# A PSUM copy moved to ScalarE and a layer norm regrouped, in a fused forward-and-backward kernel

## Chip, cores, metric

The kernel runs on one core of a Trainium2 chip. The metric is the device time of one launch in microseconds, the median of several launches. Engines are named as the profile names them: PE is TensorE (matmuls), PEld its weight loads, DVE is VectorE, ACT is ScalarE, POOL is GpSimd, SP is SyncE, which here issues nearly all DMA transfers (its queue is SPq). PEclk is the granted clock of TensorE, 1.00 being full speed.

## The reference

One layer and all its gradients. A layer norm of `x` (2048 x 1024) feeds two branches: a filter branch that convolves along the sequence by Fourier transforms, and a gated MLP with a hidden size of 3584. The kernel returns the output and nine gradients.

```python
x = A_q
xn = _layernorm(x, axis=-1)                       # (x - mean) / sqrt(var + 1e-5), bf16 steps
out = x + _A_ref(xn, A_k, A_v, A_shift_k, A_ssm_k, A_ssm_D) \
        + _B_ref(xn, B_W_gate, B_W_up, B_W_down)  # h = relu(xn Wg) * (xn Wu); h Wd
# ... and jax.vjp of it with grad_out, for all inputs but B_x
```

Nothing in the reference is special to the change. What matters is the load: the MLP's products keep TensorE full for nearly 2 ms, and the filter branch is threaded through the first half of them, group of 128 channels by group.

## The kernel before

Three places matter. Each group's filter is transposed on TensorE into PSUM and copied to SBUF. The copy is the last line but one, and it is on VectorE (`vcopy`):

```python
def ttile(self, name):
    return self.ts.tile([P, 19, P], BF16, name=name, tag="ts")     # self.ts: a ring of 3 buffers

def h_tile(self, st):
    hT = self.ttile("hT")
    hv = st["hn"][:].rearrange("p r c -> p (r c)").rearrange("p (q r) -> p r q", r=16)
    pst = self.ps.tile([P, 16, P], BF16, name="pst", tag="aps")    # one of 2 PSUM buffers of the branch
    for r in range(16):
        self.pri.now()
        self.nc.tensor.transpose(pst[:, r, :], hv[:, r, :], self.identA[:])
    self.vcopy(hT[:, 0:16, :], pst[:])
    return hT
```

The layer norm is a generator that works on chunks of 1, 1, 2, 2, 2, 4 and 4 tiles of 128 rows. Its steps are interleaved with the MLP's first block. The program is traced in one order, and the queue of each engine is ordered from it when the kernel is built, by priorities and estimates; `keep_in_program_order` pins an instruction behind what was traced before it on its engine.

```python
LN_CHUNKS = (1, 1, 2, 2, 2, 4, 4)

def layer_norm(self, xn_d, jpool, jtag, spool):
    st0 = 0
    for i, n in enumerate(self.LN_CHUNKS):
        ...
        for j in range(n):
            total = row_sums(j, 0, ACT.Copy)          # on ACT
            if i >= 3 and j == 0:
                self.tc.keep_in_program_order(total)
        mean = average(0, b(0))                       # on DVE
        if i == 2:
            self.tc.keep_in_program_order(mean)       # <- this pin matters below
        V.tensor_copy(out=f(1), in_=b(0))
        for j in range(n):
            V.tensor_scalar(out=xt[:, j, :], ..., op0=ALU.subtract)
            row_sums(j, 2, ACT.Square)
        yield                                         # end of step 1
        var = average(2, b(1))
        if i == 1:
            self.tc.keep_in_program_order(var)
        ...                                           # square root on ACT, six small DVE instructions
        self.ln_dve = V.reciprocal(out=self.rstd[:, st0:st0 + n], in_=f(10))
        self.pri.now()
        for j in range(n):
            V.tensor_scalar(out=xt[:, j, :], ..., op0=ALU.mult)
            ...
        yield                                         # end of step 2
```

The start of the MLP uses it so (`flip` transposes normalized tiles on TensorE and copies them from `pst_x` to `xnT` on VectorE):

```python
def chunk():
    next(ln)
    next(ln)

if ahead:
    self.warm(28)      # dummy matmuls
    chunk()            # tile 0
    next(ln)           # tile 1, step 1
    flip(1)            # tile 0: transposes and copy
    next(ln)           # tile 1, step 2
    chunk()            # tiles 2 and 3
    yield from gate_up(0)
    ...
```

## Time and profile before

| | before |
|---|---|
| median of 3 launches | 1957.82 us (1957.11 to 1959.85) |
| profiled span | 1954.1 us, at the fast end of this kernel's launches |
| PE busy | 1919.8 us (98%) |
| PE waits on the filter copy | 9.7 us, 4 times |
| PE waits in the layer norm | 4.5 us in all |

To read it: PE is the bound. The prediction below shows the list of waits. Two more views of this kernel are needed. The first is PE's timeline at the two first products of the MLP (columns: start in us, length in us, engine, line, operation, tiles, shape, count, and in brackets the idle time before it and what ended that):

```profile
11.85 1.90 PE L663 MATMUL ps_g<-wg,xnT 128*128 128x512 bf16 x8 [0.79 <-DVE ln_b L615]
...
15.83 0.39 PE L663 MATMUL ps_g<-wg,xnT 128*128 128x512 bf16 x1 [1.18 <-DVE xnT L689]
```

Tile 0's product starts at 11.85 us and takes 1.90 us for eight matmuls. The second view is the table of stretches (stretch in us, its length, busy time and count of each engine, then PEclk, DMA share and GB/s), around the wait on the filter copy that ends at 847.49:

```profile
core 0: us, PE busy (x) PEld busy (x) DVE busy (x) ACT busy (x) POOL busy (x), PEclk, DMA share, GB/s
...
847.00:850.50 3.50, 3.01 (x22) 1.61 (x22) 3.50 (x5) 1.01 (x1) 0.00 (x0) 0.52 0.09 20
```

PEclk is 0.52 in these 3.5 us: a stretch of half clock, 3.41 us long, begins at 847.11. PE not only stood still for 2.48 us, it also ran at half speed for the 3.0 us that were left of the stretch. The page's slices, 49 us wide, hide this: they show 9 everywhere.

### The profile page before, as it was taken

The page shows a single profiled execution, that of the slowest core. Times are in us where ns is not written, and L with a number is a line of the kernel's source. Part 1 is how long each engine was busy: PE and PEld are TensorE (multiplying, and loading weights), DVE is VectorE, ACT ScalarE, POOL GpSimd, SP SyncE. Part 2 cuts the span into 40 slices and gives each one's busy share as a digit, 9 for nine tenths or more (in the row PEclk, how much of TensorE's full clock was granted, in tenths as well). Part 3 has the DMA queues.
Part 4 walks back from the last instruction along what each step waited for, and adds up shares of the span by engine and source line. Part 5 has one row for each costly group of instructions (what it writes and reads, how often), then busy time and mean ns, then how long its engine had stood idle before and what let it go on. Part 6 is the DMA issues. An engine that isn't in the chain of part 4 may idle for free.

```text
span 1954.1 us, 36167 instructions
## 1 busy us (share of the span) xinstructions
PE 1919.8 (98%) x15530; PEld 884.3 (45%) x15530; DVE 913.0 (47%) x1356; ACT 617.0 (32%) x852; POOL 15.4 (1%) x38
## 2 busy tenths in 40 slices
PE   8989999999999999999999999999999999999998
PEld 4434444444444444444444444444444444444443
DVE  6767668677677566255255435300222222222222
ACT  6544454444444434434444444411000000000000
POOL 1100000000000000000000000000000000000000
PEclk9999999999999999999999999999999999999999
DMA  9975778964775874453663543592999955554451
GB/s 267 237 174 145 186 179 185 210 184 137 168 186 137 211 206 131 141 152 118 191 156 114 138 124 95 135 292 89 254 237 242 209 132 121 122 123 122 121 124 36
DMA packets 615969, 319.08 MB, mean 163 GB/s; under 512 B 450936, under 2 KB 585088, under 8 KB 615808
## 3 DMA queue, kind: packets, MB, share of 16 engines
q1 hardware_dynamic: 605312, 295.79, 60.3%
q10 hardware_dynamic: 9216, 16.78, 2.9%
q0 software_dynamic: 1280, 4.20, 0.6%
q8 instruction: 121, 1.98, 0.4%
q14 instruction: 40, 0.33, 0.1%
HBM read 141.56 MB, written 95.44 MB: 121 GB/s over the span
## 4 chain that ended last, share of the span: by engine, by line
PE 88%; DVE 5%; DMA 3%; issue 2%; SPq 1%; ACT 0%; POOL 0%; DVEq 0%; POOLq 0%; ACTq 0%
PE ps_w L810 19%; PE ps_x L944 19%; PE ps_o L910 10%; PE ps_g L663 9%; PE ps_h L663 8%; PE ps_u L663 8%; PE ps_d L810 8%; PE ps L66 6%; DVE tap L74 1%; DMA out_dram<-gv 1%; DVE flp L304 1%; DVE gk L74 1%; DVE ksh L74 1%; DMA kp<-in_A_k_dram 1%; DMA xn_nat<-xn_d 1%
## 5 line engine op out<-in xcount | busy, mean ns | idle before, releaser
L810 PE MATMUL ps_w<-ugs,xn_nat 128*128 128x512 bf16 x1792 | 400.3, 379 | 2.0 <-DMA xn_nat<-xn_d 1.6
L663 PEld LDWEIGHTS <-xnT 128*128 128x128 bf16 x1792 | 171.0, 98 | 217.6 <-issue 15.0
L810 PEld LDWEIGHTS <-xn_nat 128*128 128x128 bf16 x1792 | 170.7, 98 | 209.7 <-issue 5.9
L663 PE MATMUL ps_g<-wg,xnT 128*128 128x512 bf16 x896 | 207.5, 382 | 8.1 <-DVE ru L734 3.9
L663 PE MATMUL ps_u<-wu,xnT 128*128 128x512 bf16 x896 | 206.8, 381 | 0.0
L663 PE MATMUL ps_h<-wdT,goT 128*128 128x512 bf16 x896 | 205.5, 379 | 0.0
L957 ACT ACTIVATE w<-xn,m 128x512 f32<-128x512 bf16 x32 | 24.3, 806 | 559.5 <-issue 317.2
L944 PE MATMUL ps_x<-wgT,ggT 128*128 128x512 bf16 x896 | 198.6, 379 | 0.0
L944 PE MATMUL ps_x<-wuT,guT 128*128 128x512 bf16 x896 | 198.6, 379 | 0.0
L910 PE MATMUL ps_o<-wd,hT 128*128 128x512 bf16 x896 | 193.6, 379 | 0.0
L810 PE MATMUL ps_d<-g_nat,hs 128*128 128x512 bf16 x832 | 188.9, 382 | 0.0
L304 DVE STREAM_TRANSPOSE flp<-C 128x1024 f32<-128x1024 f32 x48 | 90.8, 1938 | 107.6 <-ACT C L70 107.6
L865 ACT CAST wi<-ps_w 128x512 bf16<-128x512 f32 x112 | 65.5, 586 | 228.7 <-PE ps_w L810 213.2
L944 PEld LDWEIGHTS <-guT 128*128 128x128 bf16 x896 | 87.7, 98 | 105.7
L944 PEld LDWEIGHTS <-ggT 128*128 128x128 bf16 x896 | 87.7, 98 | 105.7
L910 PEld LDWEIGHTS <-hT 128*128 128x128 bf16 x896 | 87.7, 98 | 105.7
L304 DVE STREAM_TRANSPOSE flp<-B 128x1024 f32<-128x1024 f32 x48 | 90.7, 1943 | 94.6 <-ACT B L70 94.6
L663 PEld LDWEIGHTS <-goT 128*128 128x128 bf16 x896 | 85.5, 98 | 103.4 <-issue 3.4
L810 PEld LDWEIGHTS <-hs 128*128 128x128 bf16 x832 | 79.3, 98 | 97.5 <-issue 6.5
L946 DVE CUSTOM_DVE_ANT_0 gx<-ps_x,gy 128x512 f32<-128x512 f32 x32 | 22.1, 692 | 214.0 <-PE ps_x L944 214.0
L749 ACT CAST gh<-ps_h 128x512 bf16<-128x512 f32 x112 | 65.2, 585 | 161.8 <-PE ps_h L663 154.3
L734 DVE SCALAR_TENSOR_TENSOR ru<-ru,ps_u 128x512 bf16<-128x512 bf16 x112 | 76.4, 682 | 83.2 <-PE ps_u L663 36.1
(166 smaller groups left out, 1485.4 us busy)
## 6 DMA issues: line engine op xcount, KB each, us to landing
ug_d<-ru SPq DMA_DIRECT2D x112, 256.0 KB, 3.1
ugs<-ug_d SPq DMA_DIRECT2D x112, 256.0 KB, 4.4
wg<-in_B_W_gate_dram SPq DMA_DIRECT2D x56, 256.0 KB, 4.3
wu<-in_B_W_up_dram SPq DMA_DIRECT2D x56, 256.0 KB, 4.0
h_d<-ht SPq DMA_DIRECT2D x112, 128.0 KB, 2.3
hs<-h_d SPq DMA_DIRECT2D x56, 256.0 KB, 4.6
out_dram<-wi SPq DMA_DIRECT2D x56, 256.0 KB, 2.5
gt<-in_grad_out_dram SPq DMA_DIRECT2D x32, 256.0 KB, 3.1
```

The costliest lines, as they stand in the source:

```text
L66: self.nc.tensor.matmul(out, lhsT=lhsT, rhs=rhs, start=start, stop=stop)
L74: self.nc.vector.tensor_tensor(out=out, in0=in0, in1=in1, op=op)
L304: self.nc.vector.transpose(out=df[:, c0:c0 + 32, :], in_=sf[:, c0:c0 + 32, :])
L663: self.nc.tensor.matmul(ps[:], lhsT=xT[:, kt * P:(kt + 1) * P], rhs=w(kt), start=(kt == 0), stop=(kt == self.DT - 1))
L734: nc.vector.scalar_tensor_tensor(out=ru[s][:, 1, :], in0=ru[s][:, 0, :], scalar=0.0, in1=ps[:], op0=ALU.is_gt, op1=ALU.mult)
L749: nc.scalar.copy(out=gh[:], in_=ps[:])
L810: self.nc.tensor.matmul(ps[:], lhsT=lhsT(st), rhs=rhs(st), start=(st == 0), stop=(st == self.ST - 1))
L865: nc.scalar.copy(out=wo[:, d, :], in_=ps[:])
L910: nc.tensor.matmul(ps[:], lhsT=hT[:, kt, :], rhs=self.wd[:, kt, oc], start=(kt == 0), stop=(kt == self.FT - 1))
L944: nc.tensor.matmul(ps[:], lhsT=T[:, kt, :], rhs=W[:, kt, oc], start=(i == 0), stop=(i == n - 1))
L946: V.tensor_tensor_reduce(out=gx[:, oc], in0=ps[:], in1=gy[:, oc], scale=1.0, scalar=0.0, op0=ALU.add, op1=ALU.add, accum_out=m[:, ob:ob + 1])
L957: nc.scalar.activation(out=w[:, oc], in_=xn[:, oc], func=ACT.Identity, scale=m[:, 5:6], bias=m[:, 4:5])
```

## The change

The intent was, first, to move the filter tile's copy to ScalarE, whose queue is emptier; second, to cut the layer norm into three traced steps, so that tile 1's chain from variance to reciprocal root is traced ahead of tile 0's copy; third, to pin less: the pins on `mean` and `var` go, and `total` of tiles 2 and 3 and the multiply of tile 1 are pinned instead.

```diff
@@ h_tile
-        self.vcopy(hT[:, 0:16, :], pst[:])
+        self.act(hT[:, 0:16, :], pst[:])
@@ layer_norm
                 total = row_sums(j, 0, ACT.Copy)
-                if i >= 3 and j == 0:
+                if i >= 2 and j == 0:
                     self.tc.keep_in_program_order(total)
-            mean = average(0, b(0))
-            if i == 2:
-                self.tc.keep_in_program_order(mean)
+            average(0, b(0))
 ... (cut)
             yield
-            var = average(2, b(1))
-            if i == 1:
-                self.tc.keep_in_program_order(var)
+            average(2, b(1))
 ... (cut)
             self.ln_dve = V.reciprocal(out=self.rstd[:, st0:st0 + n], in_=f(10))
+            yield
             self.pri.now()
             for j in range(n):
 ... (cut)
+                xn = V.tensor_scalar(out=xt[:, j, :], ..., op0=ALU.mult)
+                if i == 1:
+                    self.tc.keep_in_program_order(xn)
@@ hidden
                 def chunk():
-                    next(ln)
-                    next(ln)
+                    for _ in range(3):
+                        next(ln)
 
                 if ahead:
                     self.warm(28)
                     chunk()
+                    next(ln)
                     next(ln)
                     flip(1)
                     next(ln)
```

## The prediction

> **What bounds the kernel now.** I read the page first. Its head says that TensorE (PE) is busy 1919.8 of 1954.1 us, VectorE (DVE) 913.0 and ScalarE (ACT) 617.0, and the slices say that the granted clock is full throughout. A change that touches no matmul can therefore give back at most the time in which PE stands still: 1954.1 - 1919.8 = 34.3 us. Next I read the page's busy tenths by slice: DVE is at 6 to 8 tenths over the first half of the span, ACT at 4 to 6. So in the half where the filter branch runs, DVE is the fuller of the two helpers.
>
> ```profile
> PE 1919.8 (98%) x15530; PEld 884.3 (45%) x15530; DVE 913.0 (47%) x1356; ACT 617.0 (32%) x852; POOL 15.4 (1%) x38
> ...
> DVE  6767668677677566255255435300222222222222
> ACT  6544454444444434434444444411000000000000
> ```
>
> Then the list of who waited for whom, for PE alone (columns: engine, line, what it waited for, us in total, times, longest):
>
> ```profile
> PE ps L66 <- DVE hT L78: 9.7, 4, 2.9
> PE ps_g L663 <- DVE ru L734: 3.9, 2, 3.2
> PE ps_g L663 <- DVE xnT L689: 3.4, 3, 1.3
> ...
> PE ps_g L663 <- DVE ln_b L615: 0.8, 1, 0.8
> PE pst_x L687 <- DVE ln_x L644: 0.3, 1, 0.3
> ```
>
> The largest single item is the filter-tile copy that the change moves: 9.7 us in four waits. The layer-norm items add up to 3.4 + 0.8 + 0.3 = 4.5 us, all in the first 50 us. The rest of the 34.3 us is the start before the first matmul (1.5), the tail after the last (8.0, from the timeline's end) and a handful of waits that the change does not name.
>
> Which matmul waits for hT? Not the one that reads it. The timeline of PE around one of the four:
>
> ```profile
> 546.00 0.63 PE L66 MATMUL ps<-RB,flp 128*128 128x64 bf16 x16
> 546.47 1.89 PE L663 MATMUL ps_g<-wg,xnT 128*128 128x512 bf16 x8
> 551.24 0.63 PE L66 MATMUL ps<-RB,flp 128*128 128x64 bf16 x16 [2.88 <-DVE hT L78]
> ```
>
> The filter branch owns two PSUM buffers. The 16 transposes (pst) take one, the first half of the inverse transform (ps<-RB,flp) the other, and its second half needs the first one back, which happens only when pst has been copied out. In this group the last transpose ended at 544.44 us, but DVE, busy 10.00 of 10.00 us between 543 and 553 by the table of stretches, reached the copy at 549.97: 5.5 us in the queue, 1.22 us of work. ACT was busy 3.72 us in the same ten. The other three waits are alike: 2.77 us at 717.8, 2.48 at 847.5, 1.57 at 1130.9.
>
> **What the Trainium skill says.** "ScalarE: Activation LUTs", section "What ACT_TABLE_LOAD costs", gives an instruction with immediate scale and bias 186 ns + 0.833 ns per element. The trace agrees on the slope and is a little below on the start: evictions of 128x512 took 585 ns (gh<-ps_h) and of 128x1024 1015 ns (C<-ps), so (1015 - 585)/512 = 0.84 ns per element. "VectorE: DVE Perf Modes", section "Side-by-side: where the cycles go for N=2048 bf16", gives about 1224 ns in a 2x mode; the row of the copy has 1218 ns. "PSUM — Partial Sum Buffer", section "Engine vs sequencer instructions", calls the queues of ScalarE and VectorE strict FIFO, which is why a ready copy stood 5.5 us behind others. "Perfetto Trace Analysis", section "Optimization Strategy", says consistent bubbles can mean too little SBUF or PSUM for the next tile; four bubbles at the same matmul, released by the same copy, fit that.
>
> **The change, part by part.**
>
> Part 1, the copy on ACT. Removed: 8 x 1.218 = 9.7 us of DVE work. Added: 8 copies of 128x2048 on ACT. Extending the measured evictions, 1.015 + 1024 x 0.00084 = 1.88 us each, 15 us in all; ACT goes from 32% to about 33% busy. The instruction is 0.66 us slower, but the queue ahead of it is what counts. For each of the four waits I looked for two things: when ACT is free after the transposes end, and when the destination is free. The destination matters because hT lives in a ring of three buffers, and counting allocations shows that it always inherits the buffer of gks, so it can't be written before the last product of gks.
>
> - Waits at 551, 847 and 1131 (2.88 + 2.48 + 1.57 = 6.9 us): gks was last read at 534.9, 836.9 and 1119.0, before the transposes end (544.4, 841.1, 1125.4), and ACT is idle then (from 544.06 to 546.21, 840.69 to 843.37, until 1127.18). The copies should start about 0.2 us after the transposes and be done at 546.5, 843.2 and 1127.5, over 2 us ahead of the moment PE asks. I take all 6.9 us as gained.
> - Wait at 717.8 (2.77 us): gks is read until 714.35 because its products sat behind a store of gv. On ACT the copy can run from about 714.8, after an eviction, to 716.7, instead of ending at 717.75. I take 1.0 us as gained, 1.8 left.
> - The first copy has no queue: transposes end 91.72, DVE copies 91.97 to 93.19, and the matmul on hT starts at 93.29 with no gap. On ACT it ends at about 93.85: 0.6 us lost.
> - The other three copies were waited for by nobody and stay so.
>
> ACT is held 1.9 us at a time, which can delay an eviction of the main products. These have four PSUM buffers, each product takes 1.73 us or more, and ACT sat 0.7 to 2.9 us idle between evictions there, so I charge 0.5 us in total for it. Part 1: -6.9 - 1.0 + 0.6 + 0.5 = -6.8 us.
>
> Part 2, layer norm. No arithmetic is added or removed; a yield and the pins are moved. Before, tile 1's variance was pinned behind the copy of tile 0's transposes, and DVE shows the hole:
>
> ```profile
> 8.72 0.49 DVE L644 TENSOR_SCALAR ln_x<-ln_x,rstd 128x1024 bf16<-128x1024 bf16 x1
> 11.10 0.69 DVE L689 COPY xnT<-pst_x 128x1024 bf16<-128x1024 bf16 x1 [1.90 <-PE pst_x L687]
> 11.71 0.15 DVE L615 TENSOR_SCALAR ln_b<-ln_s 128x1 bf16<-128x1 f32 x1
> ...
> 13.49 0.49 DVE L644 TENSOR_SCALAR ln_x<-ln_x,rstd 128x1024 bf16<-128x1024 bf16 x1
> ```
>
> Its squares were summed at 9.47 us. From variance to the multiply is 13.49 - 11.71 = 1.78 us, so started at 9.56 the chain ends at 11.34: it fills the 1.90 us hole and may hold the copy of tile 0 back by 0.24. The multiply of tile 1 then falls at about 12.0 instead of 13.49. PE's transposes of tile 1 (waited 0.28) no longer wait, and its first product, after copy and transposes, starts near 15.2 instead of 15.83. This is less than 1.5 us, since PE runs the first product of tile 0 in between. Further on, the totals of tiles 2 and 3 now queue behind tile 1's root on ACT, some 0.4 us later than before, yet their squares start about 1.2 us earlier as the mean isn't behind the copies. The waits at 23.3 (1.26) and 47.0 (1.00) hang on DVE's queue and on a load whose issue is tied to an earlier store; I expect them a little shorter at best. Of 4.5 us I take 1.2 us as gained.
>
> Sum: 6.8 + 1.2 = 8.0 us, 1957.8 - 8.0 = 1949.8 us. That is 0.4%.
>
> **The rivals.**
> 1. ACT stalls at the head of its queue. In three groups gks is read past the end of the transposes (241.2, 714.4 and 989.4). If the issue order puts the copy ahead of evictions there, ACT stands until DVE is done and PE runs out of its four PSUM buffers. Worst at 698, during the change of phase: the copy could hold evictions from 702.1 to 716, and PE, which claims a fifth buffer at 707.1, would wait up to 9 us. For it: in-order engines, and an order that is fixed before the chip's real delays are known. Against: in the kernel before, the order foresaw that late product (the second transform half stands 14 us after the first). It would cancel everything: 1957 to 1960 us.
> 2. The wait only changes its name: after hT comes the eviction of the first half or the flip on DVE (0.8 us at 392.9). For it: DVE stays full in those windows, even with 1.2 us less. Then half the gain is lost: 1954 us.
> 3. The head start carries through: DVE, 9.7 us lighter, also shortens the 3.2 us wait on ru at 125.9 and the last layer-norm waits. Against: that wait follows a chain of seven taps with no copy of hT in it. 1945 us.
>
> **Range and chances.** Rival 3 gives the low end and rival 2 to partly 1 the high end: 1945 to 1956 us. The ceiling of what is touched is 9.7 + 4.5 = 14.2 us, 0.7%, and the worst rival costs about as much, so 2% (39 us) is out of reach in either direction.
>
> **What would show it.** In the profile after: eight copies hT<-pst on ACT near 1.88 us; the wait of PE on hT gone from the top of the list or under 3 us; DVE near 903 and ACT near 632 us; tile 1's root chain ahead of the copy near 11.1 us, and PE's layer-norm waits at 3 to 4 us instead of 4.5; a new gap near 93 us. I would be wrong if evictions of the main products wait for ACT (PE waiting on ru, wo or wi), if the four bubbles stay under another name, or if the new issue order moves gaps around elsewhere by several us, which I can't see from here.

## The result

| | before | after |
|---|---|---|
| median, 4 launches each, same rounds | 1958.57 us (1957.11 to 1959.85) | 1958.03 us (1956.46 to 1959.32) |
| ratio after to before | | 0.9997, 95% interval 0.998 to 1.0014 |
| profiled span | 1954.1 us | 1957.5 us |

A ratio here is the mean time of one kernel's fast launches over that of the other's from the same rounds, so not quite the ratio of the medians. The time did not move; 1949.8 was predicted, and 1958.03 lies outside the range of 1945 to 1956.

The page of the kernel after, and then PE's list of waits:

```profile
PE 1898.6 (97%) x15291; PEld 884.2 (45%) x15530; DVE 904.3 (46%) x1348; ACT 630.7 (32%) x860; POOL 15.4 (1%) x38
```

```profile
PE ps_g L662 <- DVE xnT L688: 11.3, 4, 9.1
PE ps L66 <- ACT hT L70: 4.7, 2, 3.0
...
PE ps_g L662 <- DVE ru L733: 3.7, 1, 3.7
```

DVE and ACT are where the prediction put them (903 and 632). PE's lower busy time is partly an artefact: this trace holds 239 fewer matmul records than that of before, and the missing ones turn up as "issue" waits of about 0.2 us. The waits on the filter copy (hT) fell from 9.7 to 4.7 us. But the first row is new in size: a wait of 9.1 us on an xnT copy, in a row that held 3.4 us in all before. PE's timeline says where it is:

```profile
18.97 3.42 PE L662 MATMUL ps_g<-wg,xnT 128*128 128x512 bf16 x8 [9.10 <-DVE xnT L688]
```

It is the very first product of tile 0, 7.12 us later than before (18.97 against 11.85), and its eight matmuls took 3.42 us instead of 1.90. The stretch from 15 to 22 us gives the reason for the second half of that: PEclk 0.52.

```profile
15.00:22.00 7.00, 3.03 (x8) 1.10 (x9) 3.21 (x12) 0.75 (x3) 1.73 (x3) 0.52 1.09 230
```

What kept the copy? The timeline of DVE after (columns as for PE; 128x1 forms belong to a chunk of one tile, 128x2 forms to the pair of tiles 2 and 3):

```profile
11.07 0.16 DVE L636 RECIPROCAL rstd<-ln_s 128x1 f32<-128x1 f32 x1
12.37 0.17 DVE L615 TENSOR_SCALAR ln_b<-ln_s 128x2 bf16<-128x2 f32 x1 [1.13 <-ACT ln_j L601]
...
15.58 0.17 DVE L615 TENSOR_SCALAR ln_b<-ln_s 128x2 bf16<-128x2 f32 x1 [1.92 <-ACT ln_j L601]
...
17.43 0.88 DVE L641 TENSOR_SCALAR ln_x<-ln_x,rstd 128x1024 bf16<-128x1024 bf16 x2
18.23 0.68 DVE L688 COPY xnT<-pst_x 128x1024 bf16<-128x1024 bf16 x1
18.83 0.48 DVE L641 TENSOR_SCALAR ln_x<-ln_x,rstd 128x1024 bf16<-128x1024 bf16 x1
```

Tile 1's root is ready at 11.2 us, as intended. Then DVE does not copy tile 0, whose transposes had ended by 9.9 us. It runs the whole chain of tiles 2 and 3 first, from the mean (12.37) to the multiply (17.43), and stands idle for ACT ahead of it and inside it (1.13 and 1.92 us). Tile 0's copy comes at 18.23. DVE takes its queue in order, so a ready copy stood behind instructions that were not ready.

The two waits on hT that are left are at 253.3 (1.68 us, in the second of the eight groups of channels, where before had none) and 725.2 us (3.02, in the fifth, where before had 2.77). The expectations count the groups from 0 and call these two 1 and 4. ACT and PE at the first of them:

```profile
251.39 1.87 ACT L70 COPY hT<-pst 128x2048 bf16<-128x2048 bf16 x1 [4.06 <-DVE tap L74]
```

```profile
253.31 0.63 PE L66 MATMUL ps<-RB,flp 128*128 128x64 bf16 x16 [1.68 <-ACT hT L70]
```

ACT is free for 4.06 us before the copy, and what releases it is DVE's tap, the last read of gks (250.06 to 251.28 us), whose buffer hT takes over.

A table of how far each kernel's eviction of the same product (ps_h to gh, ps_d to wo, ps_w to wi) lies behind before's shows where time comes from. It is worked out by subtracting start times of the same instruction in two profiles, in us; the two kernels on the left are those of this section, the others those of the experiments below.

| in before at | after | after, again | copy on ACT only | norm only | mean pinned | own buffer | 60 warm | copy 1 first | load early |
|---|---|---|---|---|---|---|---|---|---|
| 32.9 | +7.6 | +10.3 | 0.0 | +9.9 | +2.3 | +2.2 | +6.2 | -1.1 | -1.3 |
| 58.5 | +8.8 | +12.0 | +1.2 | +11.3 | +2.9 | +2.6 | +6.6 | +3.9 | +1.7 |
| 218.7 | +8.9 | +11.9 | +1.2 | +11.3 | +1.4 | +2.7 | +5.1 | +3.0 | +1.6 |
| 267.4 | +11.3 | +13.1 | +2.8 | +11.3 | +3.3 | +2.7 | +9.2 | +3.0 | +1.6 |
| 507.3 | +11.8 | +11.1 | +1.4 | +10.7 | +3.5 | +1.6 | +9.8 | +2.5 | +1.6 |
| 558.8 | +8.7 | +8.0 | -1.7 | +10.7 | +0.4 | -1.5 | +6.6 | -0.6 | -1.5 |
| 795.3 | +9.1 | +5.6 | -2.2 | +8.9 | +0.4 | -3.5 | +4.3 | -3.1 | -1.2 |
| 897.7 | +4.8 | +1.9 | -6.4 | +9.2 | -2.9 | -7.6 | -0.1 | -6.2 | -5.4 |
| 1177.2 | +3.4 | +0.7 | -7.3 | +9.7 | -4.3 | -9.1 | -1.5 | -7.5 | -6.7 |

In the column of after, 7.6 us are lost by 33 us. About 3 are won back at 551, 4 at 847 and 1.7 at 1131, the three waits that the prediction named. (The profiled launch of before lay at the fast end of its launches, so the columns end a few us above what the medians say.)

### The profile page after: what moved, and what is told of

The parts are those of the page before. It is cut to its first block, busy times and chain, and to the rows that moved or that the text cites. A ratio compares the mean times of both kernels' runs of the same rounds, so it can differ in the third digit from the quotient of the medians. Undisturbed runs are those within 1.5% of the kernel's fastest.

```text
span 1957.5 us, 35931 instructions
## 1 busy us (share of the span) xinstructions
PE 1898.6 (97%) x15291; PEld 884.2 (45%) x15530; DVE 904.3 (46%) x1348; ACT 630.7 (32%) x860; POOL 15.4 (1%) x38
## 4 chain that ended last, share of the span: by engine, by line
PE 90%; issue 3%; DMA 3%; DVE 2%; ACT 1%; SPq 0%; POOL 0%; DVEq 0%; ACTq 0%; POOLq 0%
PE ps_w L810 20%; PE ps_x L944 18%; PE ps_o L910 10%; PE ps_g L662 9%; PE ps_d L810 9%; PE ps_u L662 9%; PE ps_h L662 9%; PE ps L66 6%; ACT ln_j L601 1%; DMA out_dram<-gv 1%; DMA ln_x<-in_A_q_dram 1%; DMA kp<-in_A_k_dram 1%; DVE ksh L74 0%; DMA ugs<-ug_d 0%; SPq L82 0%
## 5 line engine op out<-in xcount | busy, mean ns | idle before, releaser
L810 PE MATMUL ps_w<-ugs,xn_nat 128*128 128x512 bf16 x1730 | 393.0, 381 | 7.1 <-issue 4.0
L662 PE MATMUL ps_g<-wg,xnT 128*128 128x512 bf16 x866 | 208.0, 386 | 17.1 <-DVE xnT L688 11.3
L662 PE MATMUL ps_u<-wu,xnT 128*128 128x512 bf16 x864 | 201.6, 379 | 5.0 <-issue 2.3
L810 PE MATMUL ps_d<-g_nat,hs 128*128 128x512 bf16 x801 | 183.3, 381 | 3.7 <-issue 3.1
L304 DVE STREAM_TRANSPOSE flp<-B 128x1024 f32<-128x1024 f32 x48 | 90.7, 1942 | 94.5 <-ACT B L70 94.5
```

Of the source, the lines that this page charges most:

```text
L304: self.nc.vector.transpose(out=df[:, c0:c0 + 32, :], in_=sf[:, c0:c0 + 32, :])
L662: self.nc.tensor.matmul(ps[:], lhsT=xT[:, kt * P:(kt + 1) * P], rhs=w(kt), start=(kt == 0), stop=(kt == self.DT - 1))
L810: self.nc.tensor.matmul(ps[:], lhsT=lhsT(st), rhs=rhs(st), start=(st == 0), stop=(st == self.ST - 1))
```

## The experiments

The theory: moving the copy wins several us, and the regrouped norm loses as much, because without the pin on `mean` the chain of tiles 2 and 3 was queued ahead of tile 0's copy on DVE. The rivals: the copy on ACT wins nothing (ACT blocks evictions), or the loss comes from elsewhere in the new order. Launches of before differ by up to 0.5% among each other (1955.1 to 1965.0 us over 33 launches), at mean clocks of 0.992 to 0.997; so most kernels were timed in five rounds. All results were correct. The first four kernels ran in one session with the same launches of before (median 1961.07 us), the next four in a second (1960.19), the last two in a third (1959.25).

### 1. The copy on ACT alone

```diff
 # the kernel before, with
-        self.vcopy(hT[:, 0:16, :], pst[:])
+        self.act(hT[:, 0:16, :], pst[:])
```

> The kernel before with the filter tile's copy on ScalarE and nothing else. Theory (the two parts of the change cancel: layer norm loses 7 to 9 us by the order of VectorE's queue, the copy gains the rest): 4 to 7 us faster than before, about 1952 us; layer-norm waits of PE as before (4.5 us), the wait on hT at 4 to 5 us in two groups. Rival (both parts are worth about nothing and the start's loss is caught up later by itself): within 1.5 us of before.

Measured: 1949.94 us (1947.03 to 1954.79), ratio 0.9952, interval 0.9937 to 0.9968. From PE's waits:

```profile
PE ps L66 <- ACT hT L70: 3.5, 2, 2.0
```

So the copy alone wins 0.48%, 9.4 us of 1960, with an interval of 6.3 to 12.3: more than the 4 to 7 us expected, though the interval reaches into that range. The two waits left are 1.47 us in the second group and 2.04 at 713.9.

### 2. The layer norm alone

```diff
 # the kernel after, with
-        self.act(hT[:, 0:16, :], pst[:])
+        self.vcopy(hT[:, 0:16, :], pst[:])
```

> The kernel before with the three-step layer norm and its changed pins and nothing else; the filter copy stays on VectorE. Theory: VectorE takes the whole chain of tiles 2 and 3 ahead of tile 0's copy, PE stands still about 9 us before its first real matmul, and the program is 7 to 9 us slower, about 1966 us. Rival (the loss at the start is absorbed in later waits): within 2 us of before, with shorter waits of PE between 50 and 950 us.

Measured: 1965.89 us (1964.44 to 1969.01), ratio 1.0034, interval 1.0019 to 1.0048: a loss of 6.7 us (3.7 to 9.4). From PE's waits:

```profile
PE ps_g L662 <- DVE xnT L688: 10.0, 4, 7.7
PE ps L66 <- DVE hT L78: 9.4, 4, 3.0
```

The long wait is there without the copy's move, and the four waits on hT are as they were in before. The two parts of the change are of opposite sign. Added up they give -0.14%; the whole change gave -0.03% (and +0.05% in run 5, nearer to that run's rival than to its theory of a gain of 3 us), within the intervals of the parts.

### 3. The pin on the mean put back

```diff
 # the kernel after, with
-            average(0, b(0))
+            mean = average(0, b(0))
+            if i == 2:
+                self.tc.keep_in_program_order(mean)
```

> The changed kernel with one pin put back: the mean of tiles 2 and 3 stays behind tile 1's multiply, and so behind tile 0's copy. Theory: the 9.1 us gap at 19 us shrinks to about 1 us, layer-norm waits 3 to 4 us in all, and the time is 8 to 9 us under the changed kernel, about 1950 us. Rival (the gap has another cause, such as a late weight load or a late transposed tile on PE): the gap stays over 4 us and the time stays at 1958 us.

Measured: 1950.16 us (1947.43 to 1951.57), ratio 0.9951, interval 0.9938 to 0.9964. One pinned instruction took back the whole loss. The timelines of DVE and then of PE:

```profile
10.91 0.67 DVE L690 COPY xnT<-pst_x 128x1024 bf16<-128x1024 bf16 x1
...
15.42 0.17 DVE L615 TENSOR_SCALAR ln_b<-ln_s 128x2 bf16<-128x2 f32 x1 [1.92 <-ACT ln_j L601]
...
15.91 0.68 DVE L690 COPY xnT<-pst_x 128x1024 bf16<-128x1024 bf16 x1
```

```profile
11.64 1.90 PE L664 MATMUL ps_g<-wg,xnT 128*128 128x512 bf16 x8 [0.97 <-DVE xnT L690]
...
16.65 0.42 PE L664 MATMUL ps_g<-wg,xnT 128*128 128x512 bf16 x1 [2.66 <-DVE xnT L690]
```

Tile 0's copy is back at 10.91, after tile 1's root, and its product starts at 11.64, 0.2 us ahead of before: this order is what the prediction had assumed of the change itself. But the same thing now happens to tile 1's copy in small. It sits at 15.91, behind the variance of tiles 2 and 3, for whose squares DVE stands idle for 1.92 us; PE waits 2.66 us. So the intended head start still isn't there, and the time is that of run 1, which has the old norm.

### 4. A buffer of its own for hT

```diff
 # mean_pinned, with
-        hT = self.ttile("hT")
+        self.ttile("hT")                                      # keeps the ring's order as it was
+        hT = self.lng.tile([P, 16, P], BF16, name="hT")       # a buffer of its own
```

> The kernel of the run with the mean pinned, and in addition a buffer of its own for the filter tile, outside the ring of three, whose slots rotate as before. Theory (the waits on hT that are left, 1.7 and 3.0 us, come from the last read of gks in the buffer that hT inherits): both waits fall under 0.5 us, the copies start within 0.3 us of the end of the transposes in all groups, and the time is 3 to 5 us below that of the mean pinned. Rival (ScalarE's place in its queue sets the copy's start): the copies of groups 1 and 4 stay late and the time is equal within 1 us.

Measured: 1947.76 us (1946.8 to 1950.73), ratio 0.9942, interval 0.9929 to 0.9955. No PE wait on hT is left, and each copy starts 0.04 us after its transposes. At 713 us, ACT and then PE:

```profile
712.53 1.93 ACT L70 CAST ghn<-ps 128x1024 bf16<-128x1024 f32 x2 [2.27 <-DVE tap L74]
```

```profile
713.60 0.59 PE L66 MATMUL ps<-hT,RH 128*128 128x512 bf16 x2 [2.23 <-ACT ghn L70]
```

The wait is now 2.23 us on the next tile of the same ring, ghn, for the same release by DVE's tap. In the second group the wait vanished outright (in the table, +2.7 at 218.7 and +2.7 at 267.4). By the ratios the gain over run 3, 0.09%, is inside the intervals and under the 3 to 5 us expected; only the traces show it.

### 5 and 6. After once more, and with 60 dummy matmuls

```diff
 # run 5: the kernel after, unchanged.   Run 6: the kernel after, with
-                    self.warm(28)
+                    self.warm(60)
```

> The changed kernel as it is, on the same chip and in the same rounds as the next three. Theory (the parts add up: -9.4 us for the copy, +6.6 us for layer norm, each as measured alone): about 3 us faster than before. Rival (they do not add up, the loss at the start also costs part of the copy's gain): equal to before within 1.5 us.

> The changed kernel with 60 in place of 28 warming matmuls, so that PE works until about 16 us instead of standing still from 9.9 to 19 us; the order of the other engines' queues is the same. Theory (a long wait of PE costs more than its length, since the clock falls to half for 3.4 to 6.8 us after it): tile 0's copy stays near 18.2 us, the gap shrinks to about 2 us, no half-clock stretch follows it, the first products take 1.90 us again instead of 3.42, and the time falls by 1.5 to 2 us. Rival (the wait costs its length only): equal to the changed kernel within 0.7 us.

Measured: after again 1961.74 us (1956.61 to 1963.86), ratio 1.0005, interval 0.9991 to 1.0019; with 60 dummy matmuls 1953.05 us (1952.08 to 1954.42), ratio 0.9965, interval 0.9953 to 0.9977. First the stretches of after once more, then one stretch and one line of PE's timeline of run 6:

```profile
15.00:22.00 7.00, 2.72 (x7) 1.03 (x8) 3.21 (x12) 1.06 (x3) 1.74 (x3) 0.50 1.10 192
22.00:29.00 7.00, 5.99 (x23) 2.63 (x22) 0.69 (x1) 1.46 (x3) 0.00 (x0) 0.55 1.10 226
```

```profile
15.00:22.00 7.00, 4.05 (x30) 2.15 (x28) 3.77 (x13) 1.44 (x4) 1.74 (x3) 1.00 1.06 234
```

```profile
19.06 1.25 PE L662 MATMUL ps_g<-wg,xnT 128*128 128x512 bf16 x5 [2.36 <-DVE xnT L688]
```

The first product starts at the same time in all three profiles (18.97, 19.28, 19.06), and the dummy matmuls compute nothing that is used. Yet they win something: they fill the wait, and PE then starts at full clock, where after had half clock for 6.8 us in one profile and for 13.7 us in the other. In the table run 6 is 1.4 and 4.1 us ahead of the two profiles of after at 32.9 us. This splits the loss of the norm at that point: 6.2 us are the late copy itself, 1.4 to 4.1 us the clock. The expected 1.5 to 2 us for the whole launch was too little; the ratios put it at some 8 us. The profiled launches of runs 5 and 6 differ by 2.2 us only (1954.8 and 1952.6), that of run 5 being the fastest of its six; further on, run 6 has two stretches of half clock (120.9 and 250.6 us), after has four and after again two. The launches without a profile show only their mean clock (0.996 to 0.998 in run 6, 0.990 to 0.994 in run 5), so where the rest of the 8 us lies isn't shown. (An estimate from these clocks, a mean difference of 0.004 over 1955 us, is 8 us, so the clock could account for all of it; but that is an upper bound, since half clock costs nothing while PE stands still.)

### 7. The copy on ACT and a buffer of its own, with the old norm

```diff
 # act_copy_only, with
-        hT = self.ttile("hT")
+        self.ttile("hT")
+        hT = self.lng.tile([P, 16, P], BF16, name="hT")
```

> The kernel before with the filter copy on ScalarE and a buffer of its own for the filter tile; layer norm as before. Theory: the waits on hT (3.5 us of PE with the copy alone) disappear and part of the half-clock stretches with them, about 1.5 to 3 us under the run with the copy on ScalarE alone, and 0 to 2 us under the run with own buffer and pinned mean, as the old layer norm starts PE 2 us earlier. Rival (the waits only change their name in group 4, as in the earlier run with the buffer): equal within 1 us to the copy on ScalarE alone.

Measured: 1948.93 us (1946.78 to 1952.82), ratio 0.9944, interval 0.993 to 0.9957. No wait on hT; at 715.4 us 2.51 us on ghn. This is run 4 without any of the norm's regrouping, and the time is the same (0.9942 there). The gain over run 1 (0.9952) that was expected, 1.5 to 3 us, is 1.6 us by the ratios and inside the intervals, so not shown.

### 8. The head start as intended

```diff
 # own_buffer, with the variance of tiles 2 and 3 traced and pinned behind tile 1's copy
-            average(2, b(1))
+            var = average(2, b(1))
+            if i == 2:
+                self.tc.keep_in_program_order(var)
@@ gate_up
                         flip(s + 1 if ahead and sp == 0 else sp + 2)
+                        if ahead and sp == 0 and s == 1:
+                            next(ln)
+                            next(ln)
@@ hidden
                     flip(1)
                     next(ln)
-                    chunk()
+                    next(ln)
                     yield from gate_up(0)
```

> The run with own buffer and pinned mean, with tile 1's copy also put ahead of the variance of tiles 2 and 3. Theory (what is left of the three-step layer norm's loss is the 2.7 us gap before tile 1's first product, for whose copy VectorE waits behind the variance): the gap falls under 1.2 us, the half-clock stretch after it goes, PE reaches the first down product 1 us earlier than before instead of 2.2 us later, and the time is 3 to 4 us under own buffer with pinned mean, about 1944 us. Rival (later waits of the layer norm take its place): equal within 1 us.

Measured: 1947.29 us (1946.17 to 1948.44), ratio 0.9936, interval 0.9924 to 0.9948. Now the head start is real: PE's waits for the norm in the first 30 us are 1.60, 0.79 and 1.02 us, and at 32.9 us the kernel is 1.1 us ahead of before. But by the ratios the time is only some 1.2 us under run 4, inside the intervals, where 3 to 4 us were expected; the rival, that later waits of the norm take the place, came. PE, ACT and the SP queue show where it goes, one line of each:

```profile
49.91 2.51 PE L667 MATMUL ps_g<-wg,xnT 128*128 128x512 bf16 x6 [4.96 <-DVE xnT L693]
```

```profile
42.28 1.06 ACT L602 ACTIVATE ln_j<-ln_x 128x1024 bf16<-128x1024 bf16 x1 [4.49 <-DMA ln_x<-in_A_q_dram]
```

```profile
34.79 0.39 SPq L582 DMA_DIRECT2D ln_x<-in_A_q_dram  x1
```

The load of the next four tiles is issued at 34.79 us, where before issued it at 33.12, and lands at 42.2; ACT stands for 4.49 us until it does, and PE for 4.96 later on. A load in the norm's way had been hidden by the norm's own lateness.

### 9 and 10. That load earlier, with the new norm and with the old

```diff
 # copy1_first (run 9) and act_copy_own (run 10), with
                     yield from gate_up(0)
+                    with self.tc.issue_after(self.stored.ins):
+                        load(5)                  # was: after the first grad(), two stores and a transpose later
 ... (cut: the later place then skips this one load)
```

> This is copy1_first with one more edit: the load of the 4-tile chunk of x is put ahead of one transpose and two stores of tile 2's gate/up in SyncE's order. Theory (the 4.96 us wait of TensorE at 49.9 in copy1_first comes from that load being issued at 34.8, 1.7 us later than in the kernel before, into a full queue): the load is issued 2 to 3 us earlier, the wait falls to 1 to 2 us, and the kernel is about 3 us under copy1_first, near 1944 to 1945, ratio to before about 0.992. Rival (the DMA engines are full from 0 to 50 us, so the order of issue moves nothing): the load lands as late, the wait stays within 1 us of 4.96, the time equals copy1_first within 1 us (ratio 0.9936).

> The same edit of the load on act_copy_own, which has the layer norm of the kernel before. There the load was already issued early enough that the wait on it is small, so both theories expect act_copy_own within 1 us (ratio 0.9944, near 1948.5); if it gains as much as load_early does (3 us), the load bounds this stretch whatever the layer norm, and the head start of the pinned norm isn't what it serves.

Measured: run 9 1947.2 us (1945.07 to 1949.23), ratio 0.9937, interval 0.9923 to 0.9951; run 10 1948.05 us (1944.89 to 1952.67), ratio 0.9944, interval 0.993 to 0.9959. PE and ACT of run 9 at the same place:

```profile
46.44 3.63 PE L667 MATMUL ps_g<-wg,xnT 128*128 128x512 bf16 x16 [1.76 <-DVE xnT L693]
```

```profile
38.79 1.06 ACT L602 ACTIVATE ln_j<-ln_x 128x1024 bf16<-128x1024 bf16 x1 [1.28 <-DMA ln_x<-in_A_q_dram]
```

Locally the theory held. The load was issued at 31.83 us, 3.0 us earlier, ACT's wait fell to 1.28 us and PE's from 4.96 to 1.76, as expected; the rival, that full DMA engines would make the order of issue irrelevant, falls. For the launch the theory missed: the time is that of copy1_first, not 3 us less. In the table the advantage is 2.1 us at 58.5 (unrounded) and 1.4 at 218.7, and at 795.3 it has turned into a deficit of 1.9. Before the end of the last product, load_early has four stretches of half clock (127.1, 379.7, 714.2 and 922.4 us), copy1_first two (50.2 and 118.5). One place where it goes shows in the traces: the wait on ghn near 714 us is 2.99 us here against 1.67 there, followed by a stretch of half clock that copy1_first does not have. Waits of this kind vary with how the two branches meet, and nothing here controls that. Run 10 has the ratio of act_copy_own, 0.9944, as both of its theories expected: with the old norm PE's wait at that place was 0.48 us already and fell to 0.36.

The best versions are copy1_first and load_early, 0.64% and 0.63% under before; act_copy_own, with three changed lines and the old norm, is at 0.56%, inside their intervals.

## Why the prediction was wrong

**The copy on ACT: mechanism right, sum mis-sized in its terms, total right within the error, in part by luck.** Predicted -6.8 us, measured alone -9.4 (interval -12.3 to -6.3). The misses below cancel: 2.1 us too little for three waits, 1.6 and 0.5 too much for two others.
- Length: 1.88 us predicted, 1.87 measured. The three waits at 551, 847 and 1131 went away, as predicted.
- Their worth was put at 6.9 us, their bare idle time. By the table, in the column of the copy alone (with rows between those printed), they gave 3.1, 4.1 and 1.8 us, 9.0 in all. At 847 the 2.48 us of wait brought 4.1, because the half clock after it went too (PEclk 0.52). The step that failed is reading the page's slices as "the granted clock is full throughout"; with it falls the ceiling of 34.3 us for a change that touches no matmul. (A slip without consequence: DVE's 6 to 8 tenths hold for the first 16 of the 40 slices, with one 5 among them; the next four show 2, 5, 5 and 2.)
- "The other three copies were waited for by nobody and stay so" failed for the second group. hT takes over gks's buffer, and the copy on ACT waits for DVE's last read of it. The prediction had counted that buffer and named 241.2 us in its first rival, but checked only the four waits against it. It cost 1.6 us there. At 717.8 us 1.0 us was expected and 0.5 came; there the prediction had counted the late read. Run 4 shows the cause: with its own buffer the wait in the second group is gone.
- The charges were small, as guessed: the first copy cost 0.2 us rather than 0.6 (the offset goes from 1.24 at 90.7 us to 1.46 at 103.8). The big stall of rival 1, ACT blocking the main products for up to 9 us, did not come.

**The layer norm: the step that failed.** Predicted -1.2 us, measured alone +6.7. The prediction said that tile 1's chain "fills the 1.90 us hole and may hold the copy of tile 0 back by 0.24". Tile 1's chain did end where it said (11.23 against 11.34 us). But the prediction read the removed pin on `mean` as only a gain ("their squares start about 1.2 us earlier as the mean isn't behind the copies") and never asked what that pin had kept in place. It was what held the chain of tiles 2 and 3 behind tile 0's copy. Without it the whole chain went ahead, with two idle stretches in it, and held the copy back by 7.1 us (from 11.10 to 18.23), not 0.24. Run 3 shows it: that pin alone, put back, returns the copy to 10.91 us and the time to 0.9951. Why the build put an idle-prone chain of six us ahead of a copy that was ready stays open; run 6, with 60 dummy matmuls instead of 28, kept that order (the copy at 18.32 us).

**A cost that the prediction didn't count at all** is the clock after a wait: 1.4 to 4.1 us of the loss at the head is this (run 6). A wait had been priced by its length alone. When a wait brings this stretch can be worked out from the traces. In all twelve, every change of the granted clock between its first rise and the end of the last product lies on a grid of 3.41 us (to within 0.01 us), and half clock fills whole cells of that grid. Where PE, running at full clock, stood idle for 2.0 us or more within one cell, the next cell was at half clock in 32 of 32 cases; with 1.7 to 2.0 us idle in 7 of 18, with 1.0 to 1.7 in 5 of 72, with less in none. So in before the wait of 2.88 us at 551, which a boundary at 550.15 cuts into 1.79 and 1.09 us, was followed by full clock, and the shorter one at 847, with 2.10 us in one cell, by half. (The idle times are the profile's; missing matmul records lengthen some.)

**The rivals.** None of the three described what came. The prediction's list of what would make it wrong did, in its last clause: "if the new issue order moves gaps around elsewhere by several us, which I can't see from here". With the norm's loss of 6.7 in place of a gain of 1.2, the prediction's own sum reads -6.8 + 6.7 = -0.1 us, and -0.5 us was measured. The time lies in the range of rival 1 (1957 to 1960 us), but that is luck: its stall of ACT didn't happen. Rival 2's change of name was seen in run 4 (ghn for hT, 2.23 us).

**Still open**: why the build ordered DVE's queue so without the pin, and where the part of run 6's 8 us lies that isn't at the head.

## What to carry to other kernels

A pin in a tuned kernel is there for a reason: before taking it out, ask of every instruction traced after it whether it could now pass something that TensorE waits for, and whether it will stand idle there. Moving a PSUM copy to the engine with the shorter queue can pay even where that engine takes half as long again for it, but check what its destination buffer waits for in each repetition and not only in those that hurt today. And price a wait of TensorE as its length plus the half-clock stretch that may follow it: 3.4 us long, it costs 1.7 us if it is full of matmuls (an estimate; at 847 us 4.1 us came back for a wait of 2.48). Whether it follows depends here on how much of the idle time falls into one cell of the 3.41 us grid, not on the wait's length alone.

## What the Trainium skill lacked or had wrong

- "TensorE: Matmul & The Clock Gate" of the Trainium skill, section "Why this matters for your kernels", advises against PE-idle gaps above about 3 us, since the clock then falls back to half. The fall is there, but the limit is too generous as a rule: in before, half clock came with a wait of 2.48 us (0.52 from 847.0 to 850.5), while in copy1_first a wait of 2.94 us at 130.5 was followed by full clock (1.00 from 130.5 to 134.0), so the length of one gap does not decide it. In these traces 2.0 us of idle time within one cell of the 3.41 us grid was enough in 32 of 32 cases. After one long wait two or four such cells in a row ran at half clock (6.8 and 13.7 us in two profiles of the same kernel); between leaving such a wait empty and filling it with dummy matmuls lay 0.4% of the launch, of which 1.4 to 4.1 us are seen at that place.
- In no page did we find the effect that cost most here: a ready copy 7.1 us behind a chain that was queued ahead of it when the kernel was built (18.23 against 11.10 us), set off by a single unpinned instruction.
